# Fewer, larger loads at both ends of a decoding-attention kernel

## The chip, the core and the metric

The kernel runs on one core of one Trainium2 chip. The metric is the device time of one execution in microseconds (us), the median of several runs. A kernel is one program of five engines with queues of their own: PE (matrix products), DVE (vectors), ACT (scalar functions), POOL (here: constants, and passing semaphores on) and SP (here: issuing DMA loads). DMA transfers run on 16 DMA engines.

## What is computed

Two branches on one token `x` (1 x 512) are mixed by a gate. Branch A is attention of 32 heads over a cache of 16384 keys and values of 128 elements; branch B is a small gated MLP. All inputs are bf16.

```python
def _A_ref(x, k_cache, v_cache, wq, wo):          # H = 32, Sk = 16384, Dh = 128
    q = (x @ wq).reshape(B, Sq, H, Dh).transpose(0, 2, 1, 3)
    scores = jnp.einsum('bhqd,bhkd->bhqk', q, k_cache) * Dh ** (-0.5)
    p = _softmax(scores, axis=-1)
    o = jnp.einsum('bhqk,bhkd->bhqd', p, v_cache)
    return o.transpose(0, 2, 1, 3).reshape(B, Sq, H * Dh) @ wo

def _B_ref(x, w_in, w_sp, b_sp, w_out):
    z = _gelu(x @ w_in)
    z1, z2 = z[..., :Fh], _layernorm(z[..., Fh:])
    g = w_sp * z2 + b_sp                          # one token: w_sp is one number
    return (z1 * g) @ w_out

g = _sigmoid((x * gate_w).sum(-1, keepdims=True))
return g * _A_ref(...) + (1 - g) * _B_ref(...)
```

The K and V caches are 134 MB each; wq and wo are 4.2 MB each, w_in 1.8 MB, w_out 0.9 MB.

## The kernel before

**Tiling.** Two heads make a pair; there are 16 pairs (`NP`). One K or V load of a pair is 8.4 MB: 128 partitions (64 for each head) of 64 KB. Three such buffers (`buf[0..2]`) are used in turn. The loads alternate K0, K1, V0, K2, V1, K3, ..., V14, V15; the n-th goes to buffer n % 3 and waits on SP for the user of the load three places earlier. The buffer of V0 first holds wq, w_in and w_out (`setup`), so V0 waits for the last product of branch B (`w_free`). The buffer after V15 takes wo.

**The head.** SP issues wq as two loads (L292), partitions 0 to 15 and then 16 to 127, 32 KB in each partition, then w_in (L293), w_out (L295), K0 in two halves (`K_CUTS`, L642) and K1. ACT issues x, gate_w and two single numbers on its own DMA queue (L283 to L288). PE multiplies x with ones, takes the gate's sum (L324), then runs the four steps of x @ w_in (L348, waits on w_in), the queries from wq (L106, `pe_queries`, waits on `ld_q`), and later the product with w_out (`pe_mixer`). DVE and ACT do gelu, layer norm and gate between them; DVE's work on K starts after them in its queue.

**Barrier.** Every engine passes a barrier at the program's start. `open_late` moves the barrier of SP and ACT behind their first loads: behind two on SP, one on ACT.

**A pair.** DVE multiplies a quarter of K with the query at a time (L581, in place, four per pair, 4.42 us each); it takes `k_s` ahead of quarters 0 and 2. PE sums over the 128 elements with identity matmuls (L498, L91), DVE reduces what is left (L566), ACT takes the exponential (L594), and that frees the K buffer. For V, PE runs eight tiles (`values`, L106 on `p_t`), each taking one unit of `v_s`; ACT copies the sums out (L603), PE folds them (L533), and that frees the V buffer. POOL waits for each load and passes it on (`hand`): two units of `k_s` for a K, eight of `v_s` for a V.

**The tail.** V15 comes in three pieces (`V_CUTS`, in units of which 256 are a whole V: 160, 64, 32) that give 5, 2 and 1 of PE's tiles. Then the output is normalized (L674), transposed (L678), rearranged (L682) and cast to `o2` (L685). wo has 32 rows of 512 in each partition and comes in pieces of 16, 8, 4, 2, 1 and 1 (`WO_CUTS`, L647). The first 24 rows (`WIDE`) go the wide way: tiles of eight rows (`WG`), four products beside each other in the PE array (L106 on `o`), each tile taking one unit of `wo_s` from POOL; ACT then copies the four partial sums out of PSUM (L716, `d_sb`), and one product with ones adds them up. The other rows are added one by one, two products each (`add`, L721). The product with ones stands in PE's queue behind rows 24 to 27 and ahead of 28 to 31:

```python
    for j, (a, b) in enumerate(zip(WO_CUTS[:-1], WO_CUTS[1:])):
        for k in range(max(a, WIDE), b):
            y_ok = add(o2[:, k:k + 1], wo[:, k * D:(k + 1) * D],
                       [(ld_o[j], 16)] if k == a else (), k == H - 1)
        if b == 28:
            add(ones_f[:, 0:1], d_sb[:, :], [w_ok])
```

DVE and ACT cast the result (L736), and SP stores it (L740).

The functions that the change touches:

Of the kernel before, what the change touches and what calls it, by code (L numbers as in the profile page):

```python
# [12 lines left out]
P = 128  # L13
Dh = 128
H = 32
NP = H // 2
D = 512
DC = D // P
# [17 lines left out]
NT = NG // TG  # L36
ZB = F // 4
K_CUTS = (0, 128, 256)
V_CUTS = (0, 160, 224, 256)
WO_CUTS = (0, 16, 24, 28, 30, 31, 32)  # L40
WIDE = 24
inv_sqrt_dh = float(Dh) ** -0.5


# [114 lines left out]
            todo.append(i)  # L159


def open_late(nc, queue, loads):

    kind = queue.eng.engine
    blocks = {b.name: b for b in nc.m.functions[0].blocks}
    first = nc.m.functions[0].blocks[0].instructions
    at = next(j for j, i in enumerate(first) if i.engine == kind and isinstance(i, mybir.InstDrain))
    barrier = [i for i in first[at:] if i.engine == kind][:2]
    assert isinstance(barrier[1], mybir.InstEventSemaphore)
    todo = blocks[queue.name].instructions  # L170
    for i in barrier:
        first.remove(i)
    n = next(j for j, i in enumerate(todo) if not isinstance(i, mybir.InstDMACopy))
    assert n >= loads
    todo[loads:loads] = barrier


def gated_mix_kernel(nc, A_x, A_k_cache, A_v_cache, A_wq, A_wo, B_x, B_w_in, B_w_sp, B_b_sp,
                     B_w_out, gate_w, out):
    def sb(name, shape, dt):  # L180
# [7 lines left out]
    d_sb = sb("d_sb", [P, 512], FP32)  # L188
# [41 lines left out]
    wq = setup[:, 0:DC * HDh]  # L230
# [9 lines left out]
    sem = nc.alloc_semaphore  # L240
    snap = nc.snapshot_sems()
    half = sem("half")
    ld_x, ld_g, ld_q, ld_w, ld_u, st_out = (
        sem(n) for n in ("ld_x", "ld_g", "ld_q", "ld_w", "ld_u", "st_out"))
    ld_k = [sem(f"ld_k{b}") for b in range(2)]
    ld_v = [sem(f"ld_v{b}") for b in range(2)]
    ld_kf = [sem(f"ld_kf{b}") for b in range(len(K_CUTS) - 1)]
    ld_kh = [sem(f"ld_kh{b}") for b in range(len(K_CUTS) - 1)]
    ld_vp = [sem(f"ld_vp{b}") for b in range(len(V_CUTS) - 1)]
    ld_o = [sem(f"ld_o{b}") for b in range(len(WO_CUTS) - 1)]  # L250
    k_s, v_s, mul_s, red_s, sum_s, exp_s, sl_s, pv_s, drn_s, zer_s, wo_s = (
        sem(n) for n in ("k_s", "v_s", "mul_s", "red_s", "sum_s", "exp_s", "sl_s", "pv_s", "drn_s",
                         "zer_s", "wo_s"))

    ones_f = nc.const_aps.tensor(1.0, [P, P], FP32)
    ones_row = nc.const_aps.tensor(1.0, [1, P], BF16)

    pool, sp, pe, dve, act = (Queue(nc, e, n) for e, n in (
        (nc.gpsimd, "pool"), (nc.sync, "sp"), (nc.tensor, "pe"), (nc.vector, "dve"),
        (nc.scalar, "act")))  # L260
# [7 lines left out]
    def value(e, reg, top):  # L268
# [6 lines left out]
        out=ident[:, :], in_=ident[:, :], compare_op=ALU.not_equal, fill=1.0, base=0,  # L275
        pattern=[[-1, P]], channel_multiplier=1))
    for t in [L_sb, p_t, zero]:
# [6 lines left out]
           inc=(ld_x, 16))  # L284
    act.op(lambda e: e.dma_start(out=gw_row[:, :], in_=gate_w.rearrange("(a d) -> a d", a=1)),
           inc=(ld_g, 16))
    act.op(lambda e: e.dma_start(out=wb_row[:, 0:1], in_=B_w_sp), inc=(ld_g, 16))
    act.op(lambda e: e.dma_start(out=wb_row[:, 1:2], in_=B_b_sp.rearrange("(a d) -> a d", a=1)),  # L288
           inc=(ld_g, 16))
    wq_src = A_wq.rearrange("(p c) n -> p (c n)", c=DC)  # L290
    for a, b in ((0, 16), (16, P)):
        sp.op(lambda e, a=a, b=b: e.dma_start(out=wq[a:b], in_=wq_src[a:b]), inc=(ld_q, 16))  # L292
    sp.op(lambda e: e.dma_start(out=w_in, in_=B_w_in.rearrange("(p c) f -> p (c f)", c=DC)),  # L293
          inc=(ld_w, 16))
    sp.op(lambda e: e.dma_start(out=w_out, in_=B_w_out.rearrange("(p k) n -> p (k n)", k=FhC)),  # L295
          inc=(ld_u, 16))


    for c in range(DC):
# [10 lines left out]
        out=sel[:, :].rearrange("h (i x) -> h i x", x=P + 1)[:, :, 0:P:4],  # L310
        in_=ident[0:H, 0:H].unsqueeze(1).broadcast_to([H, 4, H])), wait=[const_ok, ident_ok],
        mark=True)
    dve.op(lambda e: e.tensor_reduce(
        out=pick[:, :].rearrange("p (r s) -> p s r", r=4),
        in_=ident[:, :].rearrange("p (g x) -> p x g", x=32)[:, 0:8, :]
# [42 lines left out]

    def pe_queries(e):
        e.wait_ge(*g_free)  # L360
        e.wait_ge(ld_q, 32)
        wq4 = wq.rearrange("p (c n j s d) -> p c n j s d", c=DC, n=4, s=2, d=Dh)
        xa, wa = (counter(e, n, 0) for n in ("xq", "wq"))
        with e.Fori(0, DC) as c:
            wc = setup[:, bass.ds(c * HDh, HDh)].rearrange("p (n j s d) -> p n j s d", n=4, s=2,
                                                           d=Dh)
            start = len(nc.cur_bb.bb.instructions)
            for s in range(2):
                for n in range(4):
                    ins = matmul_on(nc, e, lambda: matmul_at(  # L370
                        nc, e, q_banks[n], 64 * s, (64, 512), xb[:, bass.ds(c * P, 64)],
                        wc[:, n, :, s, :], (xb[:, 0:64], wq4[:, 0, n, :, s, :]), again=(n > 0)),
                        [(wa, in_setup + 2 * (8 * n + s) * Dh), (xa, 0)])
                    ins.then_inc(pe.sem, 1)
            registers_first(nc, start)
            e.reg_alu(xa, xa, 2 * P, ALU.add)
            e.reg_alu(wa, wa, 2 * HDh, ALU.add)
# [4 lines left out]
    for h in range(2):  # L382
        zh = ps_all[:, 6 * h * 512:(6 * h + 2) * 512].rearrange("p (b x) -> p b x", b=2)[:, :, 0:ZB]
        dve.op(lambda e, h=h, zh=zh: e.tensor_tensor(  # L384
            out=zm[:, 2 * h * ZB:2 * (h + 1) * ZB].rearrange("p (b m k) -> p b m k", b=2, k=FhC),
# [5 lines left out]
        out=z[:, :].rearrange("p (e k) -> p e k", e=2),  # L391
        in_=zm.rearrange("p (e m k) -> p e k m", e=2, k=FhC), axis=AX.X, op=ALU.add))
    dve.chain(lambda e: e.scalar_tensor_tensor(
        out=zt[:, :], in0=z[:, :], scalar=0.044715, in1=z[:, :], op0=ALU.mult, op1=ALU.mult))
    zt_ok = dve.chain(lambda e: e.scalar_tensor_tensor(
        out=zt[:, :], in0=zt[:, :], scalar=1.0, in1=z[:, :], op0=ALU.add, op1=ALU.mult))
# [17 lines left out]
        out=var[:, :], in0=mv[:, 0:1], scalar=mv[:, 0:1], in1=mv[:, 1:2], op0=ALU.mult,  # L414
# [9 lines left out]
        out=u[:, :], in0=z2n[:, :], scalar=gm_sb[:, 0:1], in1=z[:, 0:FhC], op0=ALU.mult,  # L424
# [8 lines left out]
        out=ps_all[:, 2 * 512:6 * 512].rearrange("p (n s x) -> p n s x", n=2, s=2)[:, :, 0, :],  # L433
        in_=zero[:, :].unsqueeze(1).broadcast_to([P, 2, 512])))
# [194 lines left out]
    for i in range(NP):  # L629
        user[k_at[i]], user[v_at[i]] = used_k[i], used_v[i]  # L630
    loads = sorted([(n, "k", i) for i, n in enumerate(k_at)]
                   + [(n, "v", i) for i, n in enumerate(v_at)])
    for n, kind, i in loads:
        wait = [user[n - 3]] if n >= 3 else [w_free] if buf[n % 3] is setup else []
        src = (k_src if kind == "k" else v_src)[i]
        cuts, sems = (0, KP), [(ld_k if kind == "k" else ld_v)[i % 2]]
        if n == 0:
            cuts, sems = K_CUTS, ld_kf
        elif i == NP - 1:
            cuts, sems = (K_CUTS, ld_kh) if kind == "k" else (V_CUTS, ld_vp)  # L640
        for a, b, done in zip(cuts[:-1], cuts[1:], sems):
            sp.op(lambda e, a=a, b=b, n=n, src=src: e.dma_start(  # L642
                out=buf[n % 3][:, a * Dh:b * Dh], in_=src[:, a * Dh:b * Dh]),
                wait=wait if a == 0 else (), inc=(done, 16))
# [5 lines left out]
    def hand(e, loaded, to, n):  # L650
        e.wait_ge(loaded, 16).then_inc(to, n)
        e.nop().then_inc(loaded, -16)

    def pool_pairs(e):
        for j in range(len(ld_kf)):
            hand(e, ld_kf[j], k_s, 1)
        with e.Fori(0, NP // 2 - 1):
            hand(e, ld_k[1], k_s, 2)
            hand(e, ld_v[0], v_s, NT)
            hand(e, ld_k[0], k_s, 2)  # L660
            hand(e, ld_v[1], v_s, NT)
        for j in range(len(ld_kh)):
            hand(e, ld_kh[j], k_s, 1)
        hand(e, ld_v[0], v_s, NT)
        for j, (a, b) in enumerate(zip(V_CUTS[:-1], V_CUTS[1:])):
            hand(e, ld_vp[j], v_s, (b - a) * NT // KP)
# [21 lines left out]
    def pool_wo(e):  # L688
        e.wait_ge(*d_zero)
        e.wait_ge(*o2_ok)  # L690
        for j, (a, b) in enumerate(zip(WO_CUTS[:-1], WO_CUTS[1:])):
            if a < WIDE:
# [21 lines left out]
    pe.raw(pe_wide)  # L714
    pe.n += WIDE // WG
    w_ok = act.op(lambda e: e.copy(out=d_sb[:, :], in_=d_ps), wait=[(pe.sem, pe.n)], mark=True)  # L716


    def add(lhsT, rhs, wait, mark=False):
        for s in range(NC):  # L720
            ok = pe.op(lambda e, s=s: e.matmul(  # L721
                a_ps[32 * s:32 * s + 1, 0:DQ], lhsT=lhsT, rhs=rhs[:, s * DQ:(s + 1) * DQ],
                start=False, stop=False, skip_group_check=True), wait=wait if s == 0 else (),
                mark=mark and s == NC - 1, inc=(half, 1) if mark and s == 0 else None)
        return ok

    for j, (a, b) in enumerate(zip(WO_CUTS[:-1], WO_CUTS[1:])):
        for k in range(max(a, WIDE), b):
            y_ok = add(o2[:, k:k + 1], wo[:, k * D:(k + 1) * D],
                       [(ld_o[j], 16)] if k == a else (), k == H - 1)  # L730
        if b == 28:
            add(ones_f[:, 0:1], d_sb[:, :], [w_ok])
    for q in (dve, act):
        mine = range(NC)[:NC // 2] if q is dve else range(NC)[NC // 2:]
        for s in mine:
            ok = q.op(lambda e, s=s, copy=(q is act): (e.copy if copy else e.tensor_copy)(  # L736
                out=res[0:1, s * DQ:(s + 1) * DQ], in_=a_ps[32 * s:32 * s + 1, 0:DQ]),
# [3 lines left out]
          inc=(st_out, 16))  # L741
# [9 lines left out]
    for q in (sp, pool, act, dve, pe):  # L751
        q.issue()
    nc.switch_bb("end")
    open_late(nc, sp, 2)
    open_late(nc, act, 1)


_INS = ['A_x', 'A_k_cache', 'A_v_cache', 'A_wq', 'A_wo', 'B_x', 'B_w_in', 'B_w_sp', 'B_b_sp', 'B_w_out', 'gate_w']
# [30 lines left out]
```

## Time and profile before

| | us |
|---|---|
| median of 3 runs | 660.81 (660.62 to 661.12) |
| the profiled execution's own time | 661.12 |
| its span (first to last instruction) | 659.7 |

| engine | busy us | share of the span |
|---|---|---|
| PE | 428.8 | 65% |
| DVE | 336.0 | 51% |
| ACT | 45.8 | 7% |
| POOL | 2.1 | 0% |
| DMA queue of SP | | 99.6% of 16 engines |

The loads are 279.58 MB, 424 GB/s over the span. The profile describes one execution, so its durations are to be set against its own 659.7 and 661.12 us. A share of busy time is an average over the head, the sixteen pairs and the tail, which need not have the same limit; each is to be read by itself. A DMA engine counts as busy while a packet of its is under way, whether that packet moves fast or slowly.

### The profile page before, as it was taken

To read this page: it belongs to the slowest core of one execution; us is meant where nothing else is said; L and a number is where in the kernel's file an instruction comes from. 1 tells how busy PE (TensorE), PEld (TensorE's weight loads), DVE (VectorE), ACT (ScalarE), POOL (GpSimd) and SP (SyncE) were. 2 spreads that over 40 slices of the span, in tenths; PEclk is the share of its full clock that TensorE was granted. 3 is DMA by queue.
4 is the path that set the end of the run, shared out by engine and by line. 5 is a ranking of instruction groups with operands and counts; after the bars stand their busy time and mean duration, and the time that the engine had idled before them with its cause. 6 is when DMAs were issued, how large, how long until landed. Compare 5 with 4: busy or idle time off the path is not lost. (4 is left out here: it accounts for less than half of the span.)

```text
span 659.7 us, 7755 instructions
## 1 busy us (share of the span) xinstructions
PE 428.8 (65%) x2463; PEld 47.8 (7%) x1320; DVE 336.0 (51%) x159; ACT 45.8 (7%) x112; POOL 2.1 (0%) x10
## 2 busy tenths in 40 slices
PE   0458676747857474785747478574756857488778
PEld 0000001010100001010000100001010000101022
DVE  2187655628174561817446182654718265475600
ACT  1030100010100001010000101000010100001011
POOL 1000000000000000000000000000000000000000
PEclk9968787977969698796969879696987969798977
DMA  9999999999999999999999999999999999999998
GB/s 223 378 453 441 397 437 445 445 437 437 397 445 445 441 441 397 437 445 445 441 433 397 445 445 441 441 397 437 445 445 437 437 397 445 445 411 463 397 430 334
DMA packets 6507, 279.60 MB, mean 424 GB/s; under 512 B 743, under 2 KB 1002, under 8 KB 1386
## 3 DMA queue, kind: packets, MB, share of 16 engines
q1 hardware_dynamic: 6498, 279.58, 99.6%
q8 instruction: 1, 0.02, 0.0%
q10 hardware_dynamic: 8, 0.00, 0.0%
HBM read 279.58 MB, written 0.00 MB: 424 GB/s over the span
## 5 line engine op out<-in xcount | busy, mean ns | idle before, releaser
L581 DVE TENSOR_TENSOR bufs<-bufs,qb x64 | 281.5, 4419 | 169.2 <-DVEq L86 169.2
L91 PE MATMUL ps_all<-bufs,ident 128*128 x960 | 261.7, 427 | 0.0
L498 PE MATMUL ps_all<-bufs,ident 128*128 x64 | 28.4, 444 | 151.6 <-PEq L86 151.3
L106 PE MATMUL ps_all<-bufs,p_t 128*8 x1024 | 82.4, 396 | 30.2 <-PEq L86 20.2
L566 DVE TENSOR_REDUCE s_sb<-ps_all 128x64 f32<-128x512 f32 x64 | 44.1, 689 | 94.5 <-DVEq L86 94.5
L91 PE MATMUL ps_all<-zero,ident 128*8 128x512 bf16 (+1 forms) x147 | 58.0, 395 | 0.0
L594 ACT ACTIVATE p_t<-s_sb 64x256 f32 (+1 forms) x32 | 13.3, 415 | 437.6 <-ACTq L86 437.2
L498 PEld LDWEIGHTS ps_all<-bufs,ident 128*128 128x128 bf16 x64 | 6.3, 98 | 365.6 <-issue 365.6
L106 PEld LDWEIGHTS ps_all<-bufs,p_t 128*8 x1024 | 19.4, 83 | 163.1 <-issue 161.8
L533 PE MATMUL ps_all<-pick,d_sb 128*128 128x2 f32 x128 | 17.1, 255 | 14.7 <-PEq L86 14.7
L533 PEld LDWEIGHTS ps_all<-pick,d_sb 128*128 128x128 f32 x128 | 15.8, 193 | 22.9 <-issue 22.9
L603 ACT COPY d_sb<-ps_all 128x512 f32<-128x512 f32 x16 | 9.4, 585 | 105.4 <-ACTq L86 105.4
L324 PE MATMUL ps_all<-xgw,const-float32-1.0 1*128 1x3 f32 x2 | 0.6, 358 | 14.8 <-DVE xgw L320 14.8
L608 ACT CAST ps_all<-zero 128x512 f32<-128x512 bf16 x15 | 8.8, 589 | 1.7
L480 PE MATMUL ps_all<-zero,ident 128*128 128x512 bf16 x19 | 7.4, 389 | 0.0
L384 DVE TENSOR_TENSOR bufs<-ps_all,ident 128x896 f32<-128x896 f32 x2 | 2.1, 1086 | 9.4 <-PE ps_all L91 9.4
L671 DVE RECIPROCAL rl<-ps_all 128x32 f32<-128x32 f32 x1 | 0.4, 358 | 12.2 <-PE ps_all L554 12.2
L317 DVE TENSOR_TENSOR xg_row<-x_row,gw_row 1x512 bf16<-1x512 bf16 x1 | 0.4, 414 | 12.0 <-DMA wb_row<-in_B_b_sp_dram 12.0
L674 DVE TENSOR_TENSOR o_sb<-ps_all,rl 128x32 bf16<-128x32 f32 x1 | 0.2, 192 | 11.5 <-PE ps_all L533 11.5
L594 ACT ACTIVATION_READ_ACCUMULATOR p_t<-s_sb (+1 forms) x32 | 5.9, 185 | 0.0
L91 PE MATMUL ps_all<-bufs,xb 128*128 x12 | 5.0, 554 | 0.0
L348 PE MATMUL ps_all<-bufs,xb 128*128 x4 | 2.3, 573 | 4.1 <-DMA bufs<-in_B_w_in_dram 4.1
(76 smaller groups left out, 46.3 us busy)
## 6 DMA issues: line engine op xcount, KB each, us to landing
bufs<-in_A_k_cache_dram SPq DMA_DIRECT2D x4, 4096.0 KB, 38.3
bufs<-in_A_v_cache_dram SPq DMA_DIRECT2D x1, 5120.0 KB, 34.5
bufs<-in_A_wq_dram SPq DMA_DIRECT2D x1, 3584.0 KB, 21.3
bufs<-in_A_v_cache_dram SPq DMA_DIRECT2D x1, 2048.0 KB, 39.0
bufs<-in_A_wo_dram SPq DMA_DIRECT2D x1, 2048.0 KB, 25.4
bufs<-in_B_w_in_dram SPq DMA_DIRECT2D x1, 1792.0 KB, 24.8
bufs<-in_A_v_cache_dram SPq DMA_DIRECT2D x1, 1024.0 KB, 41.0
bufs<-in_A_wo_dram SPq DMA_DIRECT2D x1, 1024.0 KB, 27.6
```

What stands on the lines that cost most here:

```text
L91: ins = eng.matmul(out, lhsT=lhsT, rhs=rhs, **flags).ins
L106: ins = eng.matmul(bank[0:m, 0:n], lhsT=lhsT, rhs=rhs, **flags).ins
L348: if n else matmul_on(nc, e, lambda: e.matmul(args[0], lhsT=args[1], rhs=args[2], **flags), [at, (xa, 0)]))
L384: dve.op(lambda e, h=h, zh=zh: e.tensor_tensor(out=zm[:, 2 * h * ZB:2 * (h + 1) * ZB].rearrange("p (b m k) -> p b m k", b=2, k=FhC), in0=z ...
L480: e.matmul(args[0], lhsT=args[1], rhs=args[2], **flags)
L498: matmul_on(nc, e, lambda: e.matmul(s3, lhsT=ident[:, :], rhs=k3[:, :, 0:W], start=True, **flags), [(kw, 0)])
L533: ins = e.matmul(o2, lhsT=d_sb[:, r * Dh:(r + 1) * Dh], rhs=pick[:, r * 2:(r + 1) * 2], start=False, stop=False, skip_group_check=True)
L566: return e.tensor_reduce(out=s_sb[:, c * QK:(c + 1) * QK], in_=s_ps[c % 2].rearrange("p (j w) -> p j w", w=W), axis=AX.X, op=ALU.add)
L581: e.tensor_tensor(out=k3, in0=k3, in1=qi, op=ALU.mult).then_inc(mul_s, 1)
L594: e.activation(out=p_t[rows, bass.ds(at, NG * 8)].rearrange("p (t c) -> p t c", c=8)[:, :, 4 * s:4 * s + 4], in_=s_sb[rows, :].rearrange(" ...
L603: return e.copy(out=d_sb[:, :], in_=d_ps)
L608: e.copy(out=d_ps, in_=zero[:, :]).then_inc(drn_s, 1)
```

## The change

- wq is one load of 128 partitions; `pe_queries` waits for 16 on `ld_q`, not 32.
- SP's barrier stands behind one load, not two.
- K0 is one load, with the semaphore of the other even K loads; POOL hands on two units of `k_s` at once.
- V15 comes in pieces of 192 and 64 (six tiles and two).
- wo comes in pieces of 16, 11, 4 and 1 rows per partition. 16 rows go the wide way (two tiles, handed on together), 16 are added one by one, and the product with ones stands ahead of all of these in PE's queue.

```diff
 K_CUTS = (0, 128, 256)
-V_CUTS = (0, 160, 224, 256)
-WO_CUTS = (0, 16, 24, 28, 30, 31, 32)
-WIDE = 24
+V_CUTS = (0, 192, 256)
+WO_CUTS = (0, 16, 27, 31, 32)
+WIDE = 16
...
-def open_late(nc, queue, loads):
+def open_late(nc, queue):
...
-    n = next(j for j, i in enumerate(todo) if not isinstance(i, mybir.InstDMACopy))
-    assert n >= loads
-    todo[loads:loads] = barrier
+    todo[1:1] = barrier
...
-    ld_kf = [sem(f"ld_kf{b}") for b in range(len(K_CUTS) - 1)]
...
-    wq_src = A_wq.rearrange("(p c) n -> p (c n)", c=DC)
-    for a, b in ((0, 16), (16, P)):
-        sp.op(lambda e, a=a, b=b: e.dma_start(out=wq[a:b], in_=wq_src[a:b]), inc=(ld_q, 16))
+    sp.op(lambda e: e.dma_start(out=wq, in_=A_wq.rearrange("(p c) n -> p (c n)", c=DC)),
+          inc=(ld_q, 16))
...
-        e.wait_ge(ld_q, 32)
+        e.wait_ge(ld_q, 16)
...
-        if n == 0:
-            cuts, sems = K_CUTS, ld_kf
-        elif i == NP - 1:
+        if i == NP - 1:
             cuts, sems = (K_CUTS, ld_kh) if kind == "k" else (V_CUTS, ld_vp)
...
     def pool_pairs(e):
-        for j in range(len(ld_kf)):
-            hand(e, ld_kf[j], k_s, 1)
+        hand(e, ld_k[0], k_s, 2)
...
+    add(ones_f[:, 0:1], d_sb[:, :], [w_ok])
     for j, (a, b) in enumerate(zip(WO_CUTS[:-1], WO_CUTS[1:])):
         for k in range(max(a, WIDE), b):
             y_ok = add(o2[:, k:k + 1], wo[:, k * D:(k + 1) * D],
                        [(ld_o[j], 16)] if k == a else (), k == H - 1)
-        if b == 28:
-            add(ones_f[:, 0:1], d_sb[:, :], [w_ok])
...
-    open_late(nc, sp, 2)
-    open_late(nc, act, 1)
+    for q in (sp, act):
+        open_late(nc, q)
```

More of the change, by code (lines that the diff above doesn't have):

```diff
@@ L170, in open_late @@
     todo = blocks[queue.name].instructions
+    assert isinstance(todo[0], mybir.InstDMACopy)
     for i in barrier:
         first.remove(i)
-    n = next(j for j, i in enumerate(todo) if not isinstance(i, mybir.InstDMACopy))
-    assert n >= loads
-    todo[loads:loads] = barrier
+    todo[1:1] = barrier
 def gated_mix_kernel(nc, A_x, A_k_cache, A_v_cache, A_wq, A_wo, B_x, B_w_in, B_w_sp, B_b_sp,
```

## The prediction

> **What bounds the kernel now.** I read the page's time slices first. The rows are the DMA engines' busy share and what they moved:
>
> ```profile
> DMA  9999999999999999999999999999999999999998
> GB/s 223 378 453 441 397 437 445 445 437 437 397 445 445 441 441 397 437 445 445 441 433 397 445 445 441 441 397 437 445 445 437 437 397 445 445 411 463 397 430 334
> ```
>
> The DMA engines are never idle, PE is busy 65% and DVE 51% of the span: the kernel is one stream of 279.6 MB plus a tail. A microsecond taken out of the stream is a microsecond of the kernel, unless a consumer then comes late. But busy is not fast: the first slice of 16.5 us moves half of what a middle slice moves, the second is low too. So I asked for the stages of the head (columns: stretch, length, busy us of each engine, granted clock, DMA share, GB/s):
>
> ```profile
> core 0: us, PE busy (x) PEld busy (x) DVE busy (x) ACT busy (x) POOL busy (x), PEclk, DMA share, GB/s
> 0.00:5.00 5.00, 0.00 (x0) 0.00 (x0) 2.89 (x2) 2.73 (x3) 2.15 (x10) 1.00 0.98 144
> 5.00:21.00 16.00, 0.61 (x4) 0.34 (x4) 2.00 (x5) 0.31 (x1) 0.00 (x0) 1.00 0.97 242
> 21.00:26.00 5.00, 0.58 (x2) 0.49 (x2) 1.06 (x5) 0.23 (x2) 0.00 (x0) 1.00 0.94 399
> 26.00:36.00 10.00, 9.43 (x48) 1.02 (x12) 3.49 (x3) 0.00 (x0) 0.00 (x0) 1.00 1.05 452
> ```
>
> Then whose bytes those are, from the page's DMA issues (KB each, us from issue to landing):
>
> ```profile
> bufs<-in_A_k_cache_dram SPq DMA_DIRECT2D x4, 4096.0 KB, 38.3
> ...
> bufs<-in_A_wq_dram SPq DMA_DIRECT2D x1, 3584.0 KB, 21.3
> ...
> bufs<-in_B_w_in_dram SPq DMA_DIRECT2D x1, 1792.0 KB, 24.8
> ...
> bufs<-in_A_wq_dram SPq DMA_DIRECT2D x1, 512.0 KB, 7.0
> ```
>
> Issued at 0.0 and 0.4 us, the two parts of wq land at 7.0 and 21.7. w_in (128 partitions), issued at 1.25, lands at 26.05: 1.84 MB in 4.35 us, 422 GB/s. The halves of the first K, each 4 MB on 128 partitions, land at 37.9 and 47.6 by the trace: 9.7 us each, 432 GB/s. So 4 MB of wq took 20.7 us where 4 MB of K take 9.7, and the rate jumps in the very microsecond that wq ends.
>
> The other end, from the chain that ended last and the timeline (start us, us, instruction, idle before it):
>
> ```profile
> 655.28 1.02 PE ps_all L106 x6
> 656.30 0.43 PE ps_all L91
> 656.73 1.34 PE ps_all L721 x16
> ```
>
> ```profile
> 628.41 0.60 PE L106 MATMUL ps_all<-bufs,p_t 128*8 x8 [2.90 <-PEq L86]
> ...
> 634.86 0.63 PE L106 MATMUL ps_all<-bufs,p_t 128*8 x8
> ...
> 640.54 1.02 PE L106 MATMUL ps_all<-bufs,p_t 128*8 x8 [2.04 <-PEq L86]
> ...
> 647.90 0.66 PE L106 MATMUL ps_all<-bufs,p_t 128*8 x8
> ...
> 651.73 0.19 DVE L685 CAST o<-ps_all 128x32 bf16<-128x32 f32 x1 [0.35 <-PE ps_all L682]
> ...
> 656.35 0.59 ACT L716 COPY d_sb<-ps_all 128x512 f32<-128x512 f32 x1 [6.39 <-PE ps_all L106]
> ...
> 657.42 0.60 PE L721 MATMUL ps_all<-bufs,o 128*1 128x256 bf16 x8
> ```
>
> The last row of wo, issued at 629.4, lands 28.2 us later at 657.6; the output lands at 659.66. The tail after the stream is 2 us, and PE and the landings run side by side in it.
>
> [...]524 KB on 16 partitions landed at 7.0 after a start in the second microsecond, about 100 GB/s with its latency; K runs at 432. [...]in a full queue this trace shows 0.07 (last K in two halves 19.43 us, a whole K 19.35), and that I use.
>
> **The change part by part.**
>
> *wq as one load (L292).* One DMA of 128 partitions x 32 KB, the shape of half a K: 9.7 us. The 16-row load's first packet came 1.0 us after its issue, and landings trail packets by about 0.5 to 0.9 us: landing at 11.2 at best. What the trace does not show is 128 rows starting on an empty queue. The 16 first packets of the 16-row load begin within 0.36 us, some 0.024 us per row[...]. Bounds 0 and 2.2 us, I take 0.9: wq lands at 12.1, **9.6 us** earlier (7.7 to 10.5). One 0.4 us issue on SP goes; the queue behind is backlogged, so that is worth nothing.
>
> *Does the stream keep it?* w_in then lands at 16.4 and PE's four steps (L348), waiting on it now, shift with it. The small ACT-queue loads share the engines and land at 20.6 now, behind wq's packets; with wq gone by 12 they land by about 13, their 2.5 us of DVE and PE work is done by 16. The mixer that frees the buffer for the first V ends near 35.5; that V's turn in the stream comes at 57.4. No wait.
>
> *Barrier after one SP load.* SP joins it 0.4 us earlier; ACT, whose x load ends at 0.65, becomes last. POOL and DVE may begin 0.2 us earlier, hidden behind the stream.
>
> *First K whole.* DVE's first multiply waits for the whole: landing at about 38.0, so it starts near 38.4. (Unshifted, it would go from 42.26 to 48.) Queued behind it are DVE's four multiplies and reduces, 20 us, then ACT's exp, for which SP waits before the second-next K load: ready near 60, its turn in the stream at 76.7. Cost nothing, cover 16 us. POOL does one hand-over fewer. The split saved is 0.07 us.
>
> *Last V in 192 and 64.* Pieces of 160, 64 and 32 land at 640.3, 645.3 and 647.7. On the same clock, 192 lands at 642.8 and 64 at 647.65. PE starts 0.2 after the first: 643.0 in place of 640.54. Eight tiles with all data there take 6.45 us from first to last start (628.41 to 634.86), and the seventh starts after 647.65. Last tile at 649.45 in place of 647.90: **+1.55**. Everything up to the o cast follows: 653.5.
>
> *Projection.* Before, wide tiles waited for wo landings (652.6, 655.1), the third ending at 656.30. Now two wide tiles, both landed, start at 653.8 and 654.7 and end at 655.3 to 655.7. ACT's copy of 0.59 ends at 656.0 to 656.4; the ones matmul, now ahead of the row matmuls on PE, makes all of them wait for it, and takes 0.43 (656.99 to 657.42). Then 16 rows in place of 8, at 0.109 each (eight matmuls, 0.60): 15 x 0.109 + 0.27 = 1.9. End near 658.5, before 658.0. The wo pieces land at 652.5, 655.9, 657.1, 657.5, each before its rows. So the tail is **+0.5**, or +2.1 if PE has half clock there, as it did at 654 to 656. I take +0.6. Two loads fewer in wo save 0.1 on a stream that no longer decides there: nothing.
>
> *Sum* against the profiled execution (659.7 span, 661.12 with what lies around it): 659.7 - 9.6 - 0.07 + 0.6 = 650.6. The median of the runs is 660.81, 0.3 under the profiled one: 660.8 - 9.1 = **651.7 us**.
>
> **Rivals.**
>
> *The start is slow whatever the shape* (cold DMA or memory for 20 us). Then wq gains nothing, the first K delays nothing that matters, and the tail decides: +0.6 - 0.1, 661.3, slower by up to 2. Against it: 242 GB/s until 21, 430 right after, at the end of wq and not at a round time; w_in and K are first touches as well, and wo, laid out like wq at 32 KB per partition, comes in at full rate. For it: no 128-partition load in this trace starts cold. It decides if wq lands after about 21.2. Chance 0.14.
>
> *The whole load runs at part of the rate*[...]: at 300 GB/s 14 us, landing near 16.5, gain 5.2 and 656.1. Chance 0.07.
>
> *PE's tail at half clock throughout*, wide tiles 1.28 us apart (as 641.4 to 644.2): 1.6 to 2.5 more on the likeliest case, 653.5 to 654. It is inside the likeliest case's range.
>
> **How the numbers follow.** Likeliest case 0.76: 651.7, own range 649.8 (no start delay, tail +0.2) to 654. With the part-rate case, 649.5 to 657 holds 0.8. The slow start, 0.14, is left out above, with 0.03 for a loss and a gain that cancel. About 0.2%, 1.3 us, can be told from no change. Faster: 0.76 + 0.07 = 0.83; same 0.03; slower 0.14.
>
> **What would show it.** Right: one wq load of 4096 KB landing 11 to 14 us after its issue; the head at over 400 GB/s from 3 us on; w_in's matmul near 16.5; DVE's first multiply near 38.4 rather than 42.3; K landings still 38.7 us apart per pair of loads; the last V tile 1.5 us later against the stream's end; an end 2.5 us or more after the last wo landing in place of 2.0. Wrong: wq landing after 20, or a stretch under 400 GB/s at some later load, which would mean a consumer holds the queue.

## The result, and the profile after

The changed kernel takes 652.31 us in the median of six runs (651.73 to 653.12), the kernel before 660.87 in six beside it (660.62 to 661.12): ratio 0.9872, 95% interval 0.9859 to 0.9884. That is 8.6 us faster, where 9.1 was forecast. The profiled execution has a span of 651.7 and took 653.12, so it is one of the slower ones; this matters below. Line numbers are now those of the changed kernel (L578 is the former L581, L715 the former L721).

The time slices of the page: the engines are as busy as before, but the first two slices now move 383 and 466 GB/s, where they moved 223 and 378. The dip at the start is gone; the rest of the row is much the same.

```profile
DMA  9999999999999999999999999999999999999997
GB/s 383 466 414 451 451 418 418 451 451 394 442 451 447 394 447 451 430 406 451 451 422 414 451 451 406 430 451 451 394 442 451 442 394 451 451 404 432 434 422 303
```

The stages of the head (same columns as before), and then the issues of its loads (KB, us to landing):

```profile
core 0: us, PE busy (x) PEld busy (x) DVE busy (x) ACT busy (x) POOL busy (x), PEclk, DMA share, GB/s
0.00:5.00 5.00, 0.09 (x2) 0.10 (x2) 3.07 (x2) 2.77 (x3) 2.15 (x10) 1.00 0.87 315
5.00:11.00 6.00, 0.52 (x4) 0.25 (x4) 1.49 (x4) 0.27 (x1) 0.00 (x0) 1.00 1.01 437
```

```profile
bufs<-in_A_wq_dram SPq DMA_DIRECT2D x1, 4096.0 KB, 12.4
...
bufs<-in_B_w_in_dram SPq DMA_DIRECT2D x1, 1792.0 KB, 15.6
```

The load of wq moves at 437 GB/s from 5 us on, a time at which it moved at 242 before, and it is complete at 12.4 in place of 21.7. Of these 12.4 us, 9.7 are eight packets of 1.21 us on each engine; the rest is the start, as the trace has it (the first packets on the 16 engines begin between 1.0 and 1.8 us, and take 1.5 to 2.2 us each instead of 1.21), and the landing. Everything behind it moves up:

```profile
17.15 0.55 PE L345 MATMUL ps_all<-bufs,xb 128*128 x1 [3.01 <-DMA bufs<-in_B_w_in_dram]
...
38.49 8.76 DVE L578 TENSOR_TENSOR bufs<-bufs,qb  x2 [7.33 <-DVEq L86]
```

PE still waits for w_in, at 17.15 in place of 26.57. DVE now waits 7.3 us for the whole first K. The K and V loads then land 19.35 us apart as before, to the end: the last wo row lands at 648.06 in place of 657.64, 9.58 earlier. What the stream gained it kept.

The tail (start us, us, instruction, idle before it) gave some of it back:

```profile
633.47 1.02 PE L106 MATMUL ps_all<-bufs,p_t 128*8 x8 [4.45 <-PEq L86]
...
640.10 0.67 PE L106 MATMUL ps_all<-bufs,p_t 128*8 x5
...
643.94 0.19 DVE L679 CAST o<-ps_all 128x32 bf16<-128x32 f32 x1 [0.35 <-PE ps_all L676]
...
645.38 1.19 PE L106 MATMUL ps_all<-bufs,o 128*1 x8
...
646.61 0.59 ACT L710 COPY d_sb<-ps_all 128x512 f32<-128x512 f32 x1 [4.43 <-PE ps_all L106]
647.24 1.01 PE L715 MATMUL ps_all<-d_sb,const-float32-1.0 128*1 128x256 f32 x4 [0.25 <-ACT d_sb L710]
...
648.05 1.95 PE L715 MATMUL ps_all<-bufs,o 128*1 128x256 bf16 x32
```

When the last wo row lands, at 648.06, PE has just begun with the sixteen added rows; they end at 650.0, and the output lands at 651.65, 3.59 us after that row. Before it was 2.02. The columns PEclk of the stages of the tail say why this is at the long end: PE had half clock (from 644.7 to 648.1) just when the wide tiles and the product with ones ran. The profile of before had it too, from 653.2 to 656.7 under its wide tiles, and ended at 2.02 all the same.

```profile
644.00:646.00 2.00, 1.76 (x18) 0.39 (x16) 0.13 (x1) 0.00 (x0) 0.00 (x0) 0.68 0.94 392
646.00:648.00 2.00, 1.75 (x10) 0.22 (x6) 0.00 (x0) 0.59 (x1) 0.00 (x0) 0.50 0.66 248
```

### The profile page after: what moved, and what is told of

The parts are those of the page before. It is cut to its first block, busy times and chain, and to the rows that moved or that the text cites. A ratio compares the mean times of both kernels' runs of the same rounds, so it can differ in the third digit from the quotient of the medians.

```text
span 651.7 us, 7753 instructions
## 1 busy us (share of the span) xinstructions
PE 424.8 (65%) x2470; PEld 47.8 (7%) x1328; DVE 336.0 (52%) x159; ACT 45.8 (7%) x112; POOL 2.1 (0%) x10
## 5 line engine op out<-in xcount | busy, mean ns | idle before, releaser
L578 DVE TENSOR_TENSOR bufs<-bufs,qb x64 | 281.5, 4419 | 172.5 <-DVEq L86 172.5
L106 PE MATMUL ps_all<-bufs,p_t 128*8 x1024 | 79.8, 387 | 32.5 <-PEq L86 21.9
L91 PE MATMUL ps_all<-zero,ident 128*8 128x512 bf16 (+1 forms) x146 | 56.6, 388 | 0.0
L106 PE MATMUL ps_all<-bufs,u 128*1 x14 | 2.6, 372 | 3.3 <-ACT ps_all L427 2.6
L91 PE MATMUL ps_all<-bufs,xb 128*128 x12 | 4.1, 462 | 0.0
## 6 DMA issues: line engine op xcount, KB each, us to landing
bufs<-in_A_wq_dram SPq DMA_DIRECT2D x1, 4096.0 KB, 12.4
```

Of the source, the lines that this page charges most:

```text
L91: ins = eng.matmul(out, lhsT=lhsT, rhs=rhs, **flags).ins
L106: ins = eng.matmul(bank[0:m, 0:n], lhsT=lhsT, rhs=rhs, **flags).ins
L578: e.tensor_tensor(out=k3, in0=k3, in1=qi, op=ALU.mult).then_inc(mul_s, 1)
```

## The experiments

All of them start from one of the two kernels. The kernel before ran beside each set, at 660.98, 661.34 and 661.11 us.

**wq alone.** The kernel before, with one edit:

```diff
-    wq_src = A_wq.rearrange("(p c) n -> p (c n)", c=DC)
-    for a, b in ((0, 16), (16, P)):
-        sp.op(lambda e, a=a, b=b: e.dma_start(out=wq[a:b], in_=wq_src[a:b]), inc=(ld_q, 16))
+    sp.op(lambda e: e.dma_start(out=wq, in_=A_wq.rearrange(...)), inc=(ld_q, 16))
...
-        e.wait_ge(ld_q, 32)
+        e.wait_ge(ld_q, 16)
...
-    open_late(nc, sp, 2)
+    open_late(nc, sp, 1)
```

> The kernel before with one part of the change: wq as one load of 128 partitions (and so SP's barrier behind one load). First K in halves, last V in three pieces and the projection stay as before. [...]wq lands near 12.4 us as in the changed kernel instead of 21.7, the whole stream moves up by 9.3, and the tail keeps its 2.0 us: 660.9 - 9.3 = 651.6 us, some 0.7 under the changed kernel. Rival (the gain comes with the fewer loads at the ends or the whole first K): no more than 1 us gained, 660 or above.

Measured: 652.01 us (651.72 to 652.36), ratio 0.9863 (0.9848 to 0.9878). wq lands at 12.5:

```profile
bufs<-in_A_wq_dram SPq DMA_DIRECT2D x1, 4096.0 KB, 12.5
```

This one part is the whole gain. The last wo row lands at 648.45, 0.4 later than in the changed kernel (more small loads; wq itself 0.1 later), and the output 2.29 us after it.

**All but wq.** The changed kernel, with wq and SP's barrier as before (the same lines, undone).

> The changed kernel with wq in two loads of 16 and 112 partitions as before (SP's barrier behind two): all of the change but wq. [...]wq lands at 21.7, the stream is that of before less 0.1 to 0.2, and the longer tail is all that is left: 660.9 + 0.6 to 1.6 = 661.5 to 662.5, slower than before. Rival (the other parts bring the gain): near 652 to 655.

Measured: 661.9 us (661.0 to 663.57), ratio 1.0015 (1.0009 to 1.0022): slower, a little. The two wq loads are as slow as ever:

```profile
bufs<-in_A_wq_dram SPq DMA_DIRECT2D x1, 3584.0 KB, 21.0
...
bufs<-in_A_wq_dram SPq DMA_DIRECT2D x1, 512.0 KB, 6.7
```

The last wo row lands at 657.09, 0.55 earlier than before (0.3 of it in wq itself), and the output 3.78 us after it, with half clock from 654.1 to 657.5. The other edits cost some 0.9 us in the median.

**Is it two loads, or their partitions?** The changed kernel with wq in two loads of 128 partitions and 16 KB each:

```diff
+    for a, b in ((0, 2 * HDh), (2 * HDh, 4 * HDh)):
+        sp.op(lambda e, a=a, b=b: e.dma_start(out=wq[:, a:b], in_=wq_src[:, a:b]), inc=(ld_q, 16))
```

> The changed kernel with wq in two loads again, but cut by columns: 128 partitions of 16 KB, twice. [...]wq is there near 12.5, the time is that of the changed kernel, 652.3 (+0.1 for one more load). Rival (two loads at the start are slow because they are two, or because the second waits for the first): wq near 21 and about 661.

Measured: 652.62 us (651.85 to 653.31), ratio 0.9875 (0.986 to 0.989). The halves land at 7.3 and 12.2 by the trace. Two loads are harmless as such, and since SP's barrier stands behind one load here and in the next two runs too, it is not the barrier that makes wq fast or slow.

**Two loads of 64 partitions,** the same with `wq[0:64]` and `wq[64:128]`:

> The changed kernel with wq in two loads of 64 partitions. [...]each half of wq comes at about half rate (2.1 MB in 9.6 us), wq lands at 20.5 to 22 and the time is 660.5 to 662.5. Rival (only the odd number 112 is bad, or the first load of few rows): 64 divides evenly, wq lands near 12.5, 652.4.

Measured: 663.07 us (662.24 to 663.69), ratio 1.0029 (1.0018 to 1.004). The halves land at 12.9 and 22.8: 2.1 MB in 9.9 us, 212 GB/s. No run before this one had shown what 64 partitions do. An even division of the partitions is worse than the odd one of before.

**64 partitions again, but others.** wq in three loads, the first as large as before:

```diff
+    for a, b in ((32, 96), (0, 32), (96, P)):
+        sp.op(lambda e, a=a, b=b: e.dma_start(out=wq[a:b], in_=wq_src[a:b]), inc=(ld_q, 16))
```

> The changed kernel with wq in three loads: partitions 32 to 95 first, then 0 to 31, then 96 to 127. [...]the first 2.1 MB land near 7.7 us, as half of wq by columns did, not at 12.9 as partitions 0 to 63 did; each 1 MB after it takes 4.8, wq is complete near 17.4 and the time is 657 to 658. Rival (a load of fewer than 128 partitions is slow, whichever they are): first load at 12.9, wq at 22 or later, 662.5 to 663.5.

Measured: 658.12 us (657.16 to 658.56), ratio 0.9951 (0.9934 to 0.9967). The first piece in the issues of the page:

```profile
bufs<-in_A_wq_dram SPq DMA_DIRECT2D x1, 2048.0 KB, 8.5
```

Partitions 32 to 95 land at 8.5, where 0 to 63 took until 12.9; the two quarters land at 13.05 and 18.2, 4.6 and 5.1 us each for 1 MB, about 230 and 205 GB/s, again half rate. The packets, of 32 KB each, show it directly: of 32 to 95 they took 1.21 to 1.25 us from 3 to 6 us, while no other part of wq was under way, the same as in the single load; of 0 to 63 they took 2.5 to 2.6 from 3 to 10 us. The first piece is 0.8 us later than expected, which carries through to the end (the 7.7 expected for it was taken for a half by columns, which landed at 7.3). As many partitions, as many bytes, the same place in the queue: what differs is which partitions they are. No earlier run had shown that 32 to 95 would come faster than 0 to 63; why they do is not shown by this one either.

**The same in the middle of the stream.** The changed kernel with V14, 600 us after the start, in two loads; POOL waits for both:

```diff
+        if kind == "v" and i == NP - 2:
+            sp.op(lambda e, ...: e.dma_start(out=buf[n % 3][0:16], in_=src[0:16]), wait=wait, inc=(ld_v14, 16))
+            sp.op(lambda e, ...: e.dma_start(out=buf[n % 3][16:P], in_=src[16:P]), inc=(sems[0], 16))
+            continue
...
+        e.wait_ge(ld_v14, 16)
         hand(e, ld_v[0], v_s, NT)
```

> The changed kernel with its V14 load, some 600 us into the stream, cut into 16 and 112 partitions (nothing else changed; POOL waits for both). [...]the 8.4 MB land about 2.05 times as long after the load before them as otherwise (wq: 20.0 against 9.7 us), 39 to 41 us in place of 19.35, and all that follows moves by 20: 670 to 674 us. Rival (the slowness belonged to the first 20 us of a run, whatever the shape): V14 takes 19.4 us, 652.4.

Measured: 674.16 us in two runs (673.91 and 674.41), ratio 1.0195 (1.0174 to 1.0215), 21.8 more than the changed kernel. The stages while the 16 and then the 112 partitions come in, and after:

```profile
599.00:609.00 10.00, 7.78 (x35) 0.19 (x2) 6.85 (x4) 0.00 (x0) 0.00 (x0) 0.95 0.53 105
609.00:640.00 31.00, 6.37 (x27) 0.10 (x1) 4.39 (x3) 1.01 (x4) 0.00 (x0) 0.69 0.92 239
640.00:650.00 10.00, 8.42 (x80) 2.80 (x71) 0.00 (x0) 1.17 (x2) 0.00 (x0) 0.78 0.99 428
```

Slow again, on a load of another tensor some 598 us after the start, with 428 GB/s right after. The view counts a packet in the stage in which it starts, so 105 is not yet the rate of the 16 partitions, nor 0.53 the engines' share in their time. By the trace their sixteen packets of 64 KB start at 598.3 to 598.8 and end at 606.3 to 608.1: 8.0 to 9.3 us each, where a packet of 64 KB of an uncut V takes 2.4. That is 1.05 MB in 9.7 us, 108 GB/s, or 120 over the 8.7 us between landings. The 112 partitions move 7.34 MB in the 31.2 us between landings, 235 GB/s. V14 lands 39.9 us after the load before it, within the expected 39 to 41; that load itself ends 1.2 later, as its last packets run beside the first slow ones, and so the time is a little above the expected band. The rival of a slow start has fallen: it is the shape. In the stage of 239 GB/s the DMA share is 0.92, so "busy" does not show it.

**The whole first K.** The changed kernel with K0 in halves, on semaphores of their own and handed on one by one, as before:

> The changed kernel with the first K in halves again. If the whole first K is covered as the prediction has it: DVE's first multiply starts near 31.6 in place of 38.5 us, and nothing else moves but 0.07 us for one more load: 652.3 to 652.4 (within 0.3 of the changed kernel on the same chip). Rival (the later first multiply is felt later in the stream): 1 us or more faster.

Measured: 653.07 us (651.91 to 653.54), against 652.37 (651.76 to 653.69) for the changed kernel on the same chip; the two ranges overlap. DVE starts 6.6 us earlier, and the last wo row lands at 648.11 against 648.12:

```profile
31.90 8.76 DVE L579 TENSOR_TENSOR bufs<-bufs,qb  x2 [0.42 <-DVEq L86]
```

So the earlier start is worth nothing at the stream's end. What lengthens the profiled run (653.54) lies behind it, in the tail: its output lands 3.98 us after its last wo row, with half clock from 645.4 to 648.8. For the other runs, and so for the 0.7 us between the medians, this is not shown.

**The tail, by halves.** First, the changed kernel with `V_CUTS = (0, 160, 224, 256)`:

> The changed kernel with the last V in its old three pieces of 160, 64 and 32. If the later last V tile is what lengthens the tail (o cast at 644.1 instead of 642.5): wide tiles start at 643.3, when the first wo piece has landed, in place of 644.5, the 16 rows are added as they land, and the tail falls from 3.6 to 2.3 us or so, also at half clock: 651.4 to 652.0, below the changed kernel by 0.3 to 1. If the sixteen added rows are what lengthens it, whatever the start: no difference.

Measured: 651.95 us (651.91 to 652.5), ratio 0.9859 (0.9842 to 0.9875). The first wide tile starts at 643.42, 1.05 earlier, as expected. In the chain that ended last (start us, us, what) ACT's copy and then the product with ones with the sixteen rows behind it, 3.0 us with half clock until 647.8, still stand at the end:

```profile
645.76 0.59 ACT d_sb L710
646.35 0.04 issue
646.40 3.04 PE ps_all L715 x36
```

The output lands 2.86 us after the last wo row, in place of 3.59, where 2.3 or so was expected: by these two profiles, both with half clock, the earlier V tile is worth some 0.7 of the 1.6, not all of it. Then, with two V pieces, the old projection (`WO_CUTS`, `WIDE = 24`, the product with ones behind row 27):

> The changed kernel with the old projection (wo in 16, 8, 4, 2, 1, 1; 24 rows the wide way; the product with ones behind rows 24 to 27), last V in 192 and 64. If the sixteen added rows at half clock lengthen the tail: three wide tiles from 644.5, copy done by 648, four rows after it, end 0.5 to 0.8 earlier than in the changed kernel's profile: 651.6 to 652.3. If the late start alone does it: as the changed kernel, 652.3.

Measured: 651.9 us (651.59 to 652.62), ratio 0.9861 (0.9845 to 0.9878). This profile has full clock throughout its tail, 1.96 us, and its chain goes through a landing, no longer through the wide tiles and ACT's copy:

```profile
620.44 26.51 DMA bufs<-in_A_wo_dram
646.95 0.04 issue
647.00 1.66 PE ps_all L715 x20
```

With another clock than the changed kernel's first profile, it does not say what the old projection is worth at half clock. At full clock, by one profile each, it is 0.4: the last run below, also with full clock there, takes 2.33.

**Both old ends, one wq, one first K.**

> The version that the runs point to: wq and the first K as one load each, last V and projection as before. Stream as in the changed kernel plus 0.2 for four more small loads, tail of 2.0 to 2.3 as before: 651.3 to 651.9, under the changed kernel by 0.4 to 1 and under the kernel with only wq changed (652.0) by about 0.1.

Measured: 651.84 us (651.67 to 652.05), ratio 0.9858 (0.9842 to 0.9875): the lowest median, though the intervals of all of these overlap. The output lands 1.96 us after the last wo row, with half clock from 643.0 to 646.4.

**The changed kernel again.**

> The changed kernel once more, beside the two that differ from it by a microsecond or less, for a comparison on one chip: 651.7 to 653.1, with an end 2.3 us after the last wo landing where PE has its full clock in the tail and 3.6 where it has half.

Measured: 652.37 us, and the profiled run (651.92) has full clock. Its chain, and the clock of its stages:

```profile
645.18 0.63 PE ps_all L106 x8
645.81 0.02 issue
645.83 0.59 ACT d_sb L710
646.43 0.04 issue
646.47 2.39 PE ps_all L715 x36
```

```profile
644.00:646.00 2.00, 1.66 (x19) 0.26 (x16) 0.00 (x0) 0.17 (x1) 0.00 (x0) 1.00 0.93 389
646.00:648.00 2.00, 1.53 (x26) 1.09 (x28) 0.00 (x0) 0.42 (x1) 0.00 (x0) 1.00 0.66 246
```

The last wo row lands at 648.12, within 0.1 of the first profile; the output 2.33 us after it, not 3.59. So one kernel has two tails 1.3 us apart, and its ten runs have two ranges of time, 651.7 to 651.9 and 652.7 to 653.7; only one of each has a profile, so that the clock divides the others too is likely, but not shown. All eight profiles with both changed ends fit: 2.33 to 2.43 us in the three with full clock from the middle of the last V's tiles on, 3.24 to 3.98 in the four with half clock at the wide tiles, and 3.28 in the run of 32 to 95, where half clock lasted under the V tiles until 645.1. With both old ends, where twelve rows fewer are added after the product with ones, the runs stay within 0.4 us of each other, and the three profiles, all with half clock at the wide tiles, end 1.96, 2.02 and 2.29 after the last row.

## Why the prediction was right, point by point

*What bounds the kernel: right.* The stream's end moved by 9.58, and the loads between stayed 19.35 apart.

*wq: right.* 12.4 measured, 12.1 forecast; the gain 9.35 and not 9.6. That the whole stream gained 9.58, so near the forecast of 9.67, is in part luck: 0.23 came in small steps behind wq (0.11 up to the first K, 0.07 at the last V, 0.04 in wo), of which 0.07 stood in the forecast's sum. The start delay of 0.9 us in the forecast was an estimate, and its upper bound of 2.2 was shown by no trace: here all engines start within 0.8 us (1.0 to 1.8), but the first packets take up to 1 us longer than later ones (1.5 to 2.2 against 1.21). That the shape of wq's loads made them slow stood on one coincidence in the trace, the rate's jump at the end of wq; 64 partitions at 212 GB/s or with packets as fast as the single load's (1.21 to 1.25 us) by their place, and V14 at 108 and 235 GB/s, show it. The figure for the 16 rows of wq, "about 100 GB/s", was loose: their packets moved 0.52 MB from 1.0 to 5.3 us, 123 GB/s, or 88 from the first packet to the landing. The 112 partitions moved at 249 GB/s before (3.67 MB in the 14.7 us between landings) and at 235 in V14, and in the trace of before their packets of 32 KB took 1.7 to 2.4 us each where those of the single load took 1.21. Why the rate goes with the partitions of a load is not shown; how the 112 rows are dealt out to the engines was not tried and stays open.

*The rival of the slow start: wrong,* by the single load itself, by the two column halves and by V14.

*Whether the stream keeps it: right.* w_in's product starts at 17.15 (16.5 forecast), the small loads' product ends by 14.2 (16), the first V is issued at 35.0 (35.5), with its turn at 57.5.

*First K whole: right in its verdict, wrong in its cover.* DVE starts at 38.49 (38.4). But the step "four multiplies and reduces, 20 us" was too small, 25.8 in the trace (38.49 to 64.3): a reduce waits for PE, at half clock at first (until 47.4), and a table load of 1.28 stands before ACT's exp. SP issues the second-next K at 66.3, not 60, with its turn at 76.9: 10.6 us of cover were left, not 16.

*Last V: right.* The 192 piece lands at 633.3 and the last tile starts at 640.1; the forecast, moved up by 9.58, says 633.2 and 639.9.

*Projection: the term that was mis-sized.* The wide tiles start at 644.47 (644.2 forecast, moved up by 9.58); then the second takes 1.19 (0.6 to 1.0 forecast), the product with ones 0.81 (0.43), and the end of the rows is 650.0 and not 648.9. The second tile and the product with ones ran at half clock; the sixteen rows took 1.95, as forecast (1.9). The forecast of +0.6 stood for something near full clock, and its upper end, +2.1, for half; measured are +0.31 at full clock (2.33 against 2.02) and +1.57 at half. The 2.02 is no full-clock figure itself, since before had half clock at its wide tiles; what the change took away is a tail that hardly felt it. The median lies between: with 9.58 gained in the stream and 8.6 in all, the tail cost 1.0 there and not 0.6. That is 0.4 of the 0.5 us by which the forecast gain was too high; the rest is the stream.

## What to carry to other kernels

Look for stages in which the DMA engines are busy and the GB/s are low, and name the load: busy does not mean fast (0.97 busy at 242 GB/s before, 1.01 at 437 after). In this kernel loads of all 128 partitions went at full rate, 422 to 437 GB/s, cut by columns too. Loads cut by partitions did not, at the start or in mid-stream: 108 to 120 GB/s for 0 to 15, 212 for 64 to 127 and 235 to 249 for 16 to 127; of the parts tried only 32 to 95 came as the whole does, with packets of 32 KB in 1.21 to 1.25 us. At the end of a stream, what has to be done after the last landing should be little, since it is done at whatever clock PE then has (0.5 or 1.0 of full in these profiles): with four rows behind the product with ones the output landed within 2.3 us of the last wo row, with sixteen up to 4.0 after it.

## What was not expected of the hardware

In the trace of the changed kernel the first 32 KB packet of each engine took 1.5 to 2.2 us, every later one in wq's second half 1.21: some 0.7 us more at the start. And PE's granted clock in the last 15 us differs from run to run of one kernel (0.5 from 644.7 to 648.1 in one, 1.0 from 637 on in the other), worth 1.3 us at the end; what sets it was not tried.
